# A recurrence feeding two mixtures on one core: a later third group, banks by use, border decays as one row, decode in halves

## The chip, the core and the metric

The kernel is one program on one core of a Trainium2 chip. The metric is device time in microseconds (us), the median of the runs shown. The engines are TensorE (PE, with its weight load PEld), VectorE (DVE), ScalarE (ACT), GpSimd (POOL) and SyncE (SP), each with its own queue, worked through in order. All transfers here are issued from SP's queue. SBUF holds tiles of 128 partitions; sums of matmuls lie in PSUM, in eight banks of 512 fp32 numbers per partition.

## The reference

A gated linear recurrence with a complex decay makes `y`, which becomes `x` of two feed-forward layers, one behind the other:

```python
for t in range(S):                                  # B, H, S, D = 4, 8, 768, 48
    new_re = ar * S_re - ai * S_im                  # decay, its magnitude clipped at 0.999
    new_im = ar * S_im + ai * S_re
    S_re, S_im = new_re + k[t] (x) v[t], new_im
    y[t] = q[t] . S_re
x = y as 3072 tokens x 384
h = x @ w_in                                        # 384 -> 2048
g = where(h > 0, h, exp(min(h, 0)) - 1)
x = g @ w_out                                       # 2048 -> 384
h = max(x @ w1, x @ w2, x @ w3)                     # 384 -> 768
out = h @ w_out2                                    # 768 -> 384
```

## The kernel before

**Stages.** The 3072 steps are cut into 12 groups of 256, each of two chunks of 128. A group's recurrence is a chain of small operations on all engines: logarithms and angles of the decay (`sq`, `m2`, `inv1`, `inv2`, `rho`, `lnr`), their running sums by matmul (`cum_t`, `cum_l`), exponentials and sines, the rotated `q` and `k` (`emul`, `hat`), their transposes (`tr_pe`, `tr_evac` for the first three groups, DVE transposes and DMAs after these), scores (`score`, `mask`), the state handed from chunk to chunk (`gain`, `state`, `state_out`), and the output (`yout`, `x_split`). `x_split` writes the 256 tokens as a high and a low part, since each fp32 product is made of three products of such parts.

Block b of the first layer has the tokens of group b. It takes eight steps (b, j), j = 0 to 7: `h_pair` (line 699, 18 matmuls) makes 256 hidden features, `elu` and `elu_split` (ACT and DVE, lines 79, 710, 84 and 719) turn them into a high and a low part, and two steps later `o_pair` (line 742, 18 matmuls) adds them into three banks x0 to x2. When a block is done, `x2_out` copies these banks and writes them to DRAM (`x2d`). Behind all twelve blocks comes the second layer (lines 948 and 972).

**Weights.** A weight arrives as 64-bit words, and `dec1` decodes each of its 16 tiles once: three integer passes on DVE (lines 202, 206 and 209), a rounding copy on ACT (line 84) and a subtraction on DVE (line 216). Step (0, j) needs tiles 2j and 2j + 1.

**What sets the order.** The steps are in a list: three of block 0, then blocks 1 and 0 in turn, then block by block; block 2 begins at place 16. Group n's chain has a table `STEPS` of relative times from -31 to -2, and each entry becomes an event at `due[n]` + r x `a`, where `due[n]` is the place of (n, 0), and `a` the pace. An event runs when the list of steps has come to its time. A scheduler then places all instructions on their engines by these priorities and its own estimate of when each is ready.

**Banks.** x0 to x2 hold the output sums, three banks (tag h) the hidden features, and two (tag a) all sums of the recurrence. `apsum` hands the two out in strict turn; an instruction that gets a bank whose sum is still to be read waits for the reader.

**Border decays.** A chunk's state is scaled by the decay at the border to the next chunk, for which `gain` writes three rows to DRAM (`gd`): one of `em`, one of `ep`, one of a rate. They come back with heads and features exchanged (`f`, 96 x 24), and DVE multiplies them there (lines 415 and 416).

Of the kernel before, what the change touches and what calls it, by code (L numbers as in the profile page):

```python
# [20 lines left out]
P = 128  # L21
# [72 lines left out]
def tile_kernel(  # L94
# [30 lines left out]

    early, banks_a = [0, True], []

    def apsum():
# [4 lines left out]
        return apsum_a()  # L133

    def apsum_a():

        if not banks_a:
            banks_a.extend(ps.tile([P, 512], F32, tag="a", name="a", bufs=2) for _ in (0, 1))
        banks_a.reverse()
        return banks_a[0]  # L140

# [22 lines left out]
    for i in (0, 2):  # L164
        raw = at([P, 4 * P], "p", bufs=2)[:, :(4 - i) * P]
        a, b = (3 * P + 2, 7 * P + 2) if i == 0 else (8 * P + 2, 10 * P + 2)
        nc.sync.dma_start(raw, consts[:, a:b])
        nc.gpsimd.tensor_copy(sums_r[:, i + i:4 + i].rearrange("p a t -> p (a t)"), raw)
    tri_l = [sums_r[:, i] for i in (0, 1)]
# [18 lines left out]
    x2d = dp.tile([NT // P, P, NK * P], F32, name="x2d")  # L188
    gd = dp.tile([2 * NG, 3, W], F32, name="gd")

# [54 lines left out]

    s_full = [at([P, 4, P], f"s{i}") for i in (0, 1)]
    s_tiles = [s[:96] for s in s_full]
    rates = [s.rearrange("p a t -> p (a t)")[96:128, :W] for s in s_full]
    for s in s_tiles:
# [75 lines left out]
    def bslice(c):  # L325
        return slice(96, 128) if c == 0 else slice(0, 32)

    def halves(n, x, k):

        if n < TRI_R:  # L330
            return
        T["halves"] = t = at([P, 2, W], "gs", F32R)
# [5 lines left out]
    def cumsum(n, tri, tri_r, x):  # L338
        bank = apsum()
        if n < TRI_R:  # L340
            nc.tensor.matmul(bank[:, :W], lhsT=tri, rhs=x, start=True, stop=True)
            return bank
        for i in (0, 1):
            nc.tensor.matmul(  # L344
                bank[:, :W], lhsT=tri_r, rhs=T["halves"][:, i], start=i == 0, stop=i == 1
            )
        return bank

    def halves_t(n, c):
        halves(n, T["th", n][:, c, :], -0.5 / math.pi)  # L350

    def halves_l(n, c):
        halves(n, T["lnr", n][:, c, :], 1.0)

    def cum_t(n, c):
        T["tps", n, c] = cumsum(n, tri_t[c], keep_r[c], T["th", n][:, c, :])

    def nr(n, c):
        bank = T.pop(("tps", n, c))
# [26 lines left out]
    def cum_l(n, c):  # L386
        T["lps", n, c] = cumsum(n, tri_l[c].bitcast(F32), tri_l[c], T["lnr", n][:, c, :])

    def cum_lx(n, c):
        bank = T.pop(("lps", n, c))  # L390
        ep, em = at([P, W], f"ep{c}"), at([P, W], f"em{c}")
        T["ep", n, c], T["em", n, c] = ep, em
        act.activation(ep, bank[:, :W], AF.Exp)
        act.activation(em, bank[:, :W], AF.Exp, scale=-1.0)

    def rate(n):
        for c in (0, 1):
            act.activation(rates[c], T["lnr", n][bslice(1 - c), c, :], AF.Exp, scale=0.5)

    def gain(n, c):  # L400
        if ends(n, c):
            return
        n2, c2 = after(n, c)
        row, off = (P - 1, 31) if c == 0 else (0, 0)
        ci = 2 * n + c
        for i, x in enumerate((T["em", n2, c2], T["ep", n, c])):
            nc.sync.dma_start(gd[ci, i:i + 1], x[row:row + 1, :])
        nc.sync.dma_start(gd[ci, 2:3], rates[c2][off:off + 1, :])
        f = at([96, 3, H], "f", bufs=2)
        for j in (0, 1):  # L410
            T["dma"] = nc.sync.dma_start(
                f[j * D:(j + 1) * D], gd[ci].rearrange("o (h d) -> d o h", h=H)
            )
        g = at([96, H], "g", bufs=2)
        nc.vector.tensor_tensor(out=g, in0=f[:, 0], in1=f[:, 1], op=ALU.mult)
        nc.vector.tensor_tensor(out=g, in0=g, in1=f[:, 2], op=ALU.mult)
        T["g", ci] = g
# [67 lines left out]
    def tr_evac(n, c, x, hf):  # L485
        if n >= PE_TR:
            return
        act.copy(
            T["qkt", n, c][x][:, 4 * hf:4 * hf + 4],
            T.pop(("trb", n, c, x, hf))[:96, :].rearrange("p (i t) -> p i t", i=4),  # L490
        )
# [22 lines left out]
    def score(n, c, hf):  # L514
        T["sc", n, c, hf] = bank = apsum()
        kt, qt = T["kt", n, c], T["qt", n, c]
# [11 lines left out]
    def mask(n, c, hf):  # L528
        bank = T.pop(("sc", n, c, hf))
        t = at([P, 4, P], "p", bufs=2)  # L530
# [27 lines left out]
    def state_out(n, c):  # L558
        ci = 2 * n + c
        if ends(n, c):  # L560
            return
        sp = T["sps", ci][:96, :W].rearrange("p (j r e) -> p j r e", j=4, r=2)
        new = split_heads(s_tiles[(ci + 1) % 2])
# [48 lines left out]
    def x_split(n, c):  # L612
        ci = 2 * n + c
        xt = x_tile(n)
        sl = slice(c * P, (c + 1) * P)
        y = T.pop(("y", n, c))[:, :W].rearrange("p (k t) -> p k t", k=NK)
        act.copy(xt[:, 0, :, sl], y)
# [136 lines left out]
    def x2_out(b):  # L754
        t = mp.tile([P, NK, BT], F32, tag="dt", name="x2", bufs=1)
        for m in range(NK):
            act.copy(t[:, m], T["x2", b][m])
        dst = x2d[2 * b:2 * b + 2].rearrange("c p (m t) -> p m c t", m=NK)
        for m in range(NK):
            nc.sync.dma_start(dst[:, m], t[:, m].rearrange("p (c t) -> p c t", t=P))  # L760

    def dec1(f):
        if f % 2:
            t = at([P, NWB], "tb")[:, :NWA]
        else:
            t = mp.tile([P, NWA], F32, tag="dt", name="dt", bufs=1)
        w1[f] = decode(wp, raw[f], NWA, f"w{f}", t)

# [59 lines left out]
    for t in (apsum_a(), apsum_a()):  # L828
        nc.tensor.matmul(t, lhsT=zero[:, :P], rhs=zero, start=True, stop=True)

    def both(f, *a):
# [65 lines left out]
    for n in range(1, NG):  # L897
        for r in STEPS:
            for half in (0, 1):
                events.append((due[n] + (r + half / 2) * a, n, r, half))  # L900
        if n + 1 < NG:
            a = min(SPAN, due[n + 1] - due[n] + a * (-FIRST - NP)) / -FIRST
# [444 lines left out]
```

## Time and profile before

| | |
|---|---|
| median of 3 runs | 923.98 us (923.41 to 925.28) |
| profiled execution | 924.66 us, of which 922.9 is the span from first to last instruction |
| busy in the span | PE 879.2 us (95%), DVE 584.8 (63%), ACT 535.8 (58%) |
| mean granted TensorE clock | 0.985 of full speed |

Busy times are a mean over stages with different limits, so the sections below go by stage. A wait is put down to the instruction that ended it.

### The profile page before, as it was taken

What the parts mean: (1) busy time and instruction counts of PE and PEld (TensorE: products, weight loads), DVE (VectorE), ACT (ScalarE), POOL (GpSimd) and SP (SyncE); (2) the same over time, 40 slices, a digit from 0 to 9 for tenths busy, and PEclk for the clock granted to TensorE, in tenths of its full rate; (3) what the DMA queues carried; (4) which work ended last, traced back from release to release, by engine and by line L of the source; (5) the groups of instructions that cost most, each with busy time, mean ns of one, the idle gap of its engine ahead of it and who ended that gap; (6) DMA issues with size and microseconds to landing.
All of it is one profiled execution on the core that took longest, in us unless ns stands there. A gap on an engine that the chain in (4) does not pass through costs nothing.

```text
span 922.9 us, 21089 instructions
## 1 busy us (share of the span) xinstructions
PE 879.2 (95%) x8968; PEld 797.4 (86%) x8968; DVE 584.8 (63%) x952; ACT 535.8 (58%) x869; POOL 1.2 (0%) x6
## 2 busy tenths in 40 slices
PE   6577999999999999999999999999999999999996
PEld 2455989999999999999999999998898989898886
DVE  5888898877877787878786643969734141413220
ACT  7958787686867675758664533746858421211121
POOL 0000000000000000000000000000000000000000
PEclk9977999999999999999999999999999999999999
DMA  9763022443433443443343323429778210000001
GB/s 329 255 224 87 11 43 85 103 103 93 98 92 98 102 89 114 75 121 76 99 83 91 53 59 100 182 93 369 259 280 308 78 35 34 1 35 1 19 17 38
DMA packets 100655, 102.21 MB, mean 111 GB/s; under 512 B 53516, under 2 KB 83528, under 8 KB 99784
## 3 DMA queue, kind: packets, MB, share of 16 engines
q1 hardware_dynamic: 100552, 100.77, 36.6%
q8 instruction: 72, 1.18, 0.5%
q14 instruction: 31, 0.25, 0.1%
HBM read 77.06 MB, written 9.53 MB: 94 GB/s over the span
## 4 chain that ended last, share of the span: by engine, by line
PE 81%; ACT 9%; DVE 6%; issue 1%; SPq 1%; DMA 1%; DVEq 0%; ACTq 0%
PE mb L948 24%; PE x L742 19%; PE h L699 18%; PE ob L972 8%; PE a L581 4%; PE a L522 3%; ACT L79 3%; ACT aux L79 1%; PE a L549 1%; PE a L344 1%; ACT e L79 1%; SPq L508 1%; ACT m L79 1%; PE a L483 1%; ACT g L84 1%
## 5 line engine op out<-in xcount | busy, mean ns | idle before, releaser
L699 PE MATMUL h<-x,w 128*128 128x256 f32 x1728 | 231.8, 287 | 2.5 <-ACT w L84 1.4
L742 PE MATMUL x<-g,w 128*128 128x256 f32 x1728 | 230.4, 286 | 0.5 <-DVE g L719 0.5
L948 PE MATMUL mb<-xx,w 128*128 128x512 f32 x972 | 224.8, 392 | 0.0
L699 PEld LDWEIGHTS h<-x,w 128*128 128x128 f32 x1728 | 217.2, 193 | 7.1 <-ACT w L84 1.6
L742 PEld LDWEIGHTS x<-g,w 128*128 128x128 f32 x1728 | 215.1, 191 | 6.6 <-issue 3.8
L948 PEld LDWEIGHTS mb<-xx,w 128*128 128x128 f32 x972 | 182.4, 188 | 40.8
L79 ACT ACTIVATE e<-h 128x512 f32<-128x512 f32 x96 | 57.0, 594 | 91.4 <-PE h L699 91.3
L710 DVE SCALAR_TENSOR_TENSOR e<-e,h 128x512 f32<-128x512 f32 x96 | 65.3, 681 | 44.8 <-ACT e L79 44.8
L84 ACT CAST g<-e 128x512 fp32r<-128x512 f32 x96 | 59.2, 617 | 49.1 <-DVE e L710 49.0
L956 DVE TENSOR_TENSOR t<-mb,t 128x512 f32<-128x512 f32 x36 | 24.9, 690 | 97.8 <-PE mb L948 97.8
L719 DVE TENSOR_TENSOR g<-e,g 128x512 fp32r<-128x512 f32 x96 | 65.6, 684 | 28.6 <-ACT g L84 28.5
L972 PE MATMUL ob<-w,m 128*128 128x384 f32 x432 | 76.4, 337 | 0.0
L972 PEld LDWEIGHTS ob<-w,m 128*128 128x128 f32 x432 | 75.6, 188 | 0.5
L84 ACT CAST m<-t 128x512 fp32r<-128x512 f32 x36 | 22.3, 619 | 92.0 <-DVE t L957 91.9
L79 ACT ACT_TABLE_LOAD x54 | 69.3, 1283 | 1.7 <-PEq L1331 0.7
L79 ACT ACTIVATE e<-e 128x512 f32<-128x512 f32 x96 | 60.7, 632 | 2.1
L957 DVE TENSOR_TENSOR t<-mb,t 128x512 f32<-128x512 f32 x36 | 24.9, 691 | 36.1 <-PE mb L948 36.1
L522 PE MATMUL a<-qkt 96*32 96x128 f32 (+3 forms) x1536 | 38.0, 244 | 3.0 <-ACT qkt L84 2.3
L522 PEld LDWEIGHTS a<-qkt 96*32 96x32 f32 x1536 | 32.3, 112 | 9.5 <-ACT qkt L84 2.6
L84 ACT COPY o<-ob 128x384 f32<-128x384 f32 x24 | 11.4, 475 | 45.6 <-PE ob L972 45.6
L960 DVE TENSOR_TENSOR m<-t,m 128x512 fp32r<-128x512 f32 x36 | 24.9, 691 | 19.7 <-ACT m L84 19.7
L532 DVE TENSOR_TENSOR p<-a,sums_r 128x512 f32<-128x512 f32 x48 | 32.7, 683 | 7.0 <-PE a L522 5.9
(106 smaller groups left out, 923.3 us busy)
## 6 DMA issues: line engine op xcount, KB each, us to landing
qkt<-tb SPq DMA_DIRECT2D x216, 64.0 KB
raw<-in_wa_dram SPq DMA_DIRECT2D x16, 768.0 KB
again<-in_wa_dram SPq DMA_DIRECT2D x16, 768.0 KB
raw<-in_wb_dram SPq DMA_DIRECT2D x6, 1536.0 KB
v<-in_v_dram SPq DMA_DIRECT2D x24, 352.0 KB
q<-in_q_dram SPq DMA_DIRECT2D x12, 384.0 KB
k<-in_k_dram SPq DMA_DIRECT2D x12, 384.0 KB
x2d<-x SPq DMA_DIRECT2D x36, 128.0 KB
```

The lines of the kernel that those rows point to most:

```text
L79: ins = self.nc.scalar.activation(out, in_, func, **k)
L84: self.nc.scalar.copy(out, in_)
L522: nc.tensor.matmul(bank[32 * s:32 * s + 32, i * P + 32 * a:i * P + 32 * b], lhsT=k1[:, f], rhs=q1[:, a:b], start=True, stop=True, tile_pos ...
L532: nc.vector.tensor_tensor(out=t.rearrange("p (i e) t -> p i e t", e=2), in0=bank.rearrange("p (i e t) -> p i e t", i=2, e=2), in1=keep[c], ...
L581: nc.tensor.matmul(bank[32 * quad:32 * quad + 32, o * P:(o + 1) * P], lhsT=lhs, rhs=rhs, start=start, stop=stop, tile_position=(0, 32 * quad),
L699: nc.tensor.matmul(bank[:, i * BT:(i + 1) * BT], lhsT=w[:, wi, wsl], rhs=xb[b][:, xi, kk, :], start=m == 0, stop=m == 8,)
L710: nc.vector.scalar_tensor_tensor(out=e, in0=e, scalar=-1.0, in1=bank, op0=ALU.add, op1=ALU.max)
L719: nc.vector.tensor_tensor(out=g[:, 1], in0=e, in1=g[:, 0].bitcast(F32), op=ALU.subtract)
L742: nc.tensor.matmul(x2[m], lhsT=w[:, wi, wsl], rhs=g[:, gi, i * BT:(i + 1) * BT], start=j + i + s == 0 and b > 1, stop=j == NP - 1 and i == ...
L948: nc.tensor.matmul(bank, lhsT=wbt[f][:, wt, o:o + P], rhs=x[:, xi, kk].rearrange("p c t -> p (c t)"), start=m == 0, stop=m == 8,)
L956: nc.vector.tensor_tensor(out=t, in0=banks[1], in1=t, op=ALU.max)
L972: nc.tensor.matmul(bank[:, :DM], lhsT=mt[:, mi, ts], rhs=wbt[f][:, wt, NWB - DM:], start=f == 0 and s == 0, stop=f == NF2 - 1 and s == 2,)
```

## The change

- `apsum` keeps a list `live` of banks whose sums are still to be read; `take` strikes a bank off when the instruction that reads it is written. `apsum` gives the bank of the two that isn't live, and where both are, one of the three of tag h.
- The group n = 2 (the third) gets a pace of its own, `due[2] / 31`, so its first event falls on time 0 and not before it.
- `rate` writes into a tile of its own, `gt`; `gain` multiplies it by `em` and `ep` on 32 partitions (the border row is one of them), sends one row to DRAM and reads back 96 x 8.
- `halves` and `cumsum` pass their tile by a key, as do others; the running sums are the same.
- Odd and even weight tiles are decoded in the two halves of one tile (`tb`), not in two tiles.
- `x2_out` uses two tiles of the pool of `elu` (tag e), where it had one of its own of three thirds.

```diff
-        banks_a.reverse()
-        return banks_a[0]
+        b = banks_a[0] if banks_a[0] not in live else banks_a[1]
+        if b in live:
+            assert not stays, "both banks hold sums that are still to be read"
+            return ps.tile([P, 512], F32, tag="h", name="a", bufs=3)
+        banks_a.remove(b)
+        banks_a.append(b)
+        live.append(b)
+        return b
+
+    def take(*key):
+        b = T.pop(key)
+        if b in live:
+            live.remove(b)
+        return b
...
     def rate(n):
+        T["gt", n] = t = at([P, W], "gt")
         for c in (0, 1):
-            act.activation(rates[c], T["lnr", n][bslice(1 - c), c, :], AF.Exp, scale=0.5)
+            sl = bslice(1 - c)
+            act.activation(t[sl], T["lnr", n][sl, c, :], AF.Exp, scale=0.5)
...
-        row, off = (P - 1, 31) if c == 0 else (0, 0)
+        sl = bslice(c)
+        t = T["gt", n2]
+        nc.vector.tensor_tensor(out=t[sl], in0=t[sl], in1=T["em", n2, c2][sl], op=ALU.mult)
+        nc.vector.tensor_tensor(out=t[sl], in0=t[sl], in1=T["ep", n, c][sl], op=ALU.mult)
+        row = P - 1 if c == 0 else 0
         ci = 2 * n + c
-        for i, x in enumerate((T["em", n2, c2], T["ep", n, c])):
-            nc.sync.dma_start(gd[ci, i:i + 1], x[row:row + 1, :])
-        nc.sync.dma_start(gd[ci, 2:3], rates[c2][off:off + 1, :])
-        f = at([96, 3, H], "f", bufs=2)
+        nc.sync.dma_start(gd[ci], t[row:row + 1, :])
+        g = at([96, H], "g", bufs=2)
         for j in (0, 1):
             T["dma"] = nc.sync.dma_start(
-                f[j * D:(j + 1) * D], gd[ci].rearrange("o (h d) -> d o h", h=H)
+                g[j * D:(j + 1) * D, :], gd[ci].rearrange("o (h d) -> d (o h)", h=H)
             )
-        g = at([96, H], "g", bufs=2)
-        nc.vector.tensor_tensor(out=g, in0=f[:, 0], in1=f[:, 1], op=ALU.mult)
-        nc.vector.tensor_tensor(out=g, in0=g, in1=f[:, 2], op=ALU.mult)
...
     def score(n, c, hf):
-        T["sc", n, c, hf] = bank = apsum()
+        T["sc", n, c, hf] = bank = apsum(n > 0)
...
     def x2_out(b):
-        t = mp.tile([P, NK, BT], F32, tag="dt", name="x2", bufs=1)
-        for m in range(NK):
-            act.copy(t[:, m], T["x2", b][m])
         dst = x2d[2 * b:2 * b + 2].rearrange("c p (m t) -> p m c t", m=NK)
         for m in range(NK):
-            nc.sync.dma_start(dst[:, m], t[:, m].rearrange("p (c t) -> p c t", t=P))
+            if m != 1:
+                t = mp.tile([P, 2, BT], F32, tag="e", name="x2", bufs=2)
+            act.copy(t[:, m % 2], T["x2", b][m])
+            nc.sync.dma_start(dst[:, m], t[:, m % 2].rearrange("p (c t) -> p c t", t=P))
+
+    words = []
 
     def dec1(f):
-        if f % 2:
-            t = at([P, NWB], "tb")[:, :NWA]
-        else:
-            t = mp.tile([P, NWA], F32, tag="dt", name="dt", bufs=1)
-        w1[f] = decode(wp, raw[f], NWA, f"w{f}", t)
+        if not words:
+            words.append(at([P, 2, NWA], "tb"))
+        w1[f] = decode(wp, raw[f], NWA, f"w{f}", words[0][:, f % 2])
...
-                events.append((due[n] + (r + half / 2) * a, n, r, half))
+                pace = due[n] / -FIRST if n == 2 else a
+                events.append((due[n] + (r + half / 2) * pace, n, r, half))
```

How the instructions stand is shown at three places. In the changed kernel the lines below 123 have moved by 10 to 16; `m_472` before and `m_844` after are the tile of the third group's squared magnitude.

On DVE, before, these rows stand between the rotated operands of the second group's first chunk (`qh`, `kh`, with one decoding row behind them) and the third group's first operation there (`m_472`):

```order
L216 TENSOR_TENSOR w<-tb,w 128x768
L202 TENSOR_SCALAR dt<-raw 128x768
L202 TENSOR_SCALAR tb<-raw 128x768
L206 SCALAR_TENSOR_TENSOR dt<-raw,dt 128x768
L206 SCALAR_TENSOR_TENSOR tb<-raw,tb 128x768
L209 SCALAR_TENSOR_TENSOR dt<-raw,dt 128x768
L209 SCALAR_TENSOR_TENSOR tb<-raw,tb 128x768
L216 TENSOR_TENSOR w<-dt,w 128x768
L202 TENSOR_SCALAR dt<-raw 128x768
L287 TENSOR_TENSOR m_472<-aux,m_472 128x768
```

On DVE after the change, the rows behind the same two operands:

```order
L421 TENSOR_TENSOR gt<-gt,em_494 32x384
L467 TENSOR_TENSOR q<-q,ep_493 128x384
L422 TENSOR_TENSOR gt<-gt,ep_478 32x384
L467 TENSOR_TENSOR k<-k,em_494 128x384
L724 SCALAR_TENSOR_TENSOR e<-e,h 128x512
L474 TENSOR_TENSOR qh<-q,cs 128x768
L228 TENSOR_TENSOR w<-tb,w 128x768
L218 SCALAR_TENSOR_TENSOR tb<-raw,tb 128x768
L733 TENSOR_TENSOR g<-e,g 128x512
L221 SCALAR_TENSOR_TENSOR tb<-raw,tb 128x768
L474 TENSOR_TENSOR kh<-k,cs 128x768
```

The second chunk's operands and the first `elu` now stand ahead of the next tiles' decoding; `m_844` comes 15 rows further down, behind the second group's first `x_split`.

On PE, before, from the middle of the first hidden features to the second group's transposes (`cst` and `qh` or `kh`), with the state sums (`v`, `kh`) between:

```order
L699 MATMUL h<-x,w 128x256 x25
L483 MATMUL a<-cst,qh 96x128 x4
L699 MATMUL h<-x,w 128x256 x16
L549 MATMUL a<-v,kh 32x48 x13
L483 MATMUL a<-cst,qh 96x128 x4
L549 MATMUL a<-v,kh 32x48 x11
L483 MATMUL a<-cst,kh 96x128 x8
```

On PE after the change, the same place:

```order
L713 MATMUL h<-x,w 128x256 x17
L497 MATMUL a<-cst,qh 96x128 x8
L497 MATMUL a<-cst,kh 96x128 x4
L713 MATMUL h<-x,w 128x256 x2
L497 MATMUL a<-cst,kh 96x128 x4
L756 MATMUL x_119<-g,w 128x256
```

The third step's hidden matmuls no longer stand between the transposes but behind them, and the first output matmuls stand close by.

On SP, before, at the end of a later block (`x2d` is the block's output, `qkt` the next group's transposes):

```order
L265 DMA k<-in_k_dram 128x768
L760 DMA x2d<-x_2804 128x2x128 x3
L144 DMA re<-in_a_re_dram 128x768
```

On SP after the change:

```order
L275 DMA k<-in_k_dram 128x768
L774 DMA x2d<-x_2775 128x2x128 x2
L774 DMA x2d<-x_2780 128x2x128
L156 DMA re<-in_a_re_dram 128x768
```

The three writes leave from two tiles, of which the second has a place of its own in the pool of `elu`.

## Rows read from the trace of the kernel before

**Rows 1.** The page's 40 slices: busy tenths, granted clock in tenths.
```profile
PE   6577999999999999999999999999999999999996
PEclk9977999999999999999999999999999999999999
```

**Rows 2.** Windows by stage: stretch and length; busy of PE, PEld, DVE, ACT, POOL; clock, DMA.
```profile
60.00:82.50 22.50, 12.00 (x163) 9.81 (x164) 19.59 (x30) 16.53 (x24) 0.00 (x0) 0.62 0.20 35
...
95.00:172.00 77.00, 74.24 (x866) 69.78 (x865) 69.65 (x115) 63.08 (x98) 0.00 (x0) 1.00 0.20 49
...
172.00:616.50 444.50, 441.45 (x5897) 424.53 (x5896) 326.23 (x550) 284.02 (x452) 0.00 (x0) 1.00 0.38 96
616.50:923.00 306.50, 299.34 (x1406) 257.71 (x1404) 111.88 (x162) 115.90 (x214) 0.00 (x0) 0.99 0.32 115
```

**Rows 3.** Who PE waited for from 50 to 100 us: total, times, longest.
```profile
PE a L483 <- ACT em L79: 5.7, 1, 5.7
PE a L483 <- ACT qkt L84: 3.5, 2, 2.1
```

**Rows 4.** Timeline: start, length, instruction, count, idle before it and what ended that.
```profile
61.23 0.95 DVE L216 TENSOR_TENSOR w<-dt,w 128x768 fp32r<-128x768 f32 x1
...
62.10 0.95 DVE L216 TENSOR_TENSOR w<-tb,w 128x768 fp32r<-128x768 f32 x1
...
66.63 0.83 ACT L84 CAST w<-dt 128x768 fp32r<-128x768 f32 x1 [4.82 <-DVE dt L209]
67.36 0.84 ACT L79 ACTIVATE m<-re 128x768 f32<-128x768 f32 x1
...
69.67 1.28 ACT L79 ACT_TABLE_LOAD   x1
...
71.36 0.48 ACT L79 ACTIVATE em<-a 128x384 f32<-128x384 f32 x1
...
71.89 1.09 PE L483 MATMUL a<-cst,qh 128*96 128x128 f32 x4 [5.70 <-ACT em L79]
```

**Rows 5.** Windows from one DVE row to another, columns as in rows 2.
```profile
26.62:95.64 69.02, 50.08 (x793) 40.54 (x794) 61.96 (x99) 52.60 (x76) 0.00 (x0) 0.83 0.51 167
95.64:172.17 76.53, 73.77 (x861) 69.31 (x861) 69.18 (x114) 62.49 (x96) 0.00 (x0) 1.00 0.20 49
```

**Rows 6.** DVE's groups by shape: count, busy us, mean ns, idle before and its end.
```profile
L381 DVE SCALAR_TENSOR_TENSOR th<-nr,cst,th 32x384 f32<-32x384 f32 x20 | 12.2, 611 | 0.5
...
L303 DVE TENSOR_TENSOR re<-re,aux 128x768 f32<-128x768 f32 x11 | 10.5, 958 | 9.8 <-ACT aux L79 9.7
...
L415 DVE TENSOR_TENSOR g<-f 96x8 f32<-96x8 f32 x20 | 3.1, 157 | 3.6 <-DMA f<-gd 3.5 <-issue 0.2
```

**Rows 7.** Timeline: the ends and marks of the stretches, columns as in rows 4.
```profile
26.62 0.95 DVE L460 TENSOR_TENSOR qh<-q,cs 128x768 f32<-128x768 f32 x1
...
95.00 4.36 PE L699 MATMUL h<-x,w 128*128 128x256 f32 x35
...
95.64 0.69 DVE L719 TENSOR_TENSOR g<-e,g 128x512 fp32r<-128x512 f32 x1
...
168.03 0.51 DVE L618 SCALAR_TENSOR_TENSOR x<-a,x 128x384 fp32r<-128x384 f32 x1
...
170.28 2.32 PE L699 MATMUL h<-x,w 128*128 128x256 f32 x18
...
172.17 0.69 DVE L719 TENSOR_TENSOR g<-e,g 128x512 fp32r<-128x512 f32 x1
```

**Rows 8.** Timeline at the ends of two later blocks, columns as in rows 4.
```profile
229.78 0.65 ACT L84 COPY x<-x 128x256 f32<-128x256 f32 x2
229.92 0.69 DVE L719 TENSOR_TENSOR g<-e,g 128x512 fp32r<-128x512 f32 x1 [1.24 <-ACT g L84]
...
231.07 2.42 PE L742 MATMUL x<-g,w 128*128 128x256 f32 x18
...
277.17 0.69 DVE L719 TENSOR_TENSOR g<-e,g 128x512 fp32r<-128x512 f32 x1
...
278.66 2.31 PE L742 MATMUL x<-g,w 128*128 128x256 f32 x18
```

More of the change, by code (lines that the diff above doesn't have):

```diff
@@ L124, in at, with apsum @@
         return ap.tile(shape, dt, tag=tag, name=name or tag, bufs=bufs)
-    early, banks_a = [0, True], []
-    def apsum():
+    early, banks_a, live = [0, True], [], []
+    def apsum(stays=False):
         if early[1]:
@@ L132, in apsum, with apsum_a @@
                 return ps.tile([P, 512], F32, tag="h", name="a", bufs=3)
-        return apsum_a()
-    def apsum_a():
+        return apsum_a(stays)
+    def apsum_a(stays=False):
         if not banks_a:
             banks_a.extend(ps.tile([P, 512], F32, tag="a", name="a", bufs=2) for _ in (0, 1))
-        banks_a.reverse()
-        return banks_a[0]
+        b = banks_a[0] if banks_a[0] not in live else banks_a[1]
[11 more added lines that the diff above has]
+        return b
     def load_re(n):
@@ L164, in tile_kernel @@
     for i in (0, 2):
-        raw = at([P, 4 * P], "p", bufs=2)[:, :(4 - i) * P]
+        part = at([P, 4 * P], "p", bufs=2)[:, :(4 - i) * P]
         a, b = (3 * P + 2, 7 * P + 2) if i == 0 else (8 * P + 2, 10 * P + 2)
-        nc.sync.dma_start(raw, consts[:, a:b])
-        nc.gpsimd.tensor_copy(sums_r[:, i + i:4 + i].rearrange("p a t -> p (a t)"), raw)
+        nc.sync.dma_start(part, consts[:, a:b])
+        nc.gpsimd.tensor_copy(sums_r[:, i + i:4 + i].rearrange("p a t -> p (a t)"), part)
     tri_l = [sums_r[:, i] for i in (0, 1)]
@@ L188, in tile_kernel @@
     x2d = dp.tile([NT // P, P, NK * P], F32, name="x2d")
-    gd = dp.tile([2 * NG, 3, W], F32, name="gd")
+    gd = dp.tile([2 * NG, 1, W], F32, name="gd")
     def load_w(pool, src, f, n, tag):
@@ L244, in decode_any @@
         return split_w(wpool, t, n, tag)
-    s_full = [at([P, 4, P], f"s{i}") for i in (0, 1)]
-    s_tiles = [s[:96] for s in s_full]
-    rates = [s.rearrange("p a t -> p (a t)")[96:128, :W] for s in s_full]
+    s_tiles = [at([96, 4, P], f"s{i}") for i in (0, 1)]
     for s in s_tiles:
@@ L326, in bslice, with halves @@
         return slice(96, 128) if c == 0 else slice(0, 32)
-    def halves(n, x, k):
+    def halves(n, x, k, *key):
         if n < TRI_R:
             return
-        T["halves"] = t = at([P, 2, W], "gs", F32R)
+        T[key] = t = at([P, 2, W], "gs", F32R)
         nc.vector.tensor_scalar(out=t[:, 0], in0=x, scalar1=k, scalar2=None, op0=ALU.mult)
@@ L336, in halves, with cumsum @@
         )
-    def cumsum(n, tri, tri_r, x):
+    def cumsum(n, tri, tri_r, x, *key):
         bank = apsum()
@@ L342, in cumsum @@
             return bank
+        t = T.pop(key)
         for i in (0, 1):
             nc.tensor.matmul(
-                bank[:, :W], lhsT=tri_r, rhs=T["halves"][:, i], start=i == 0, stop=i == 1
+                bank[:, :W], lhsT=tri_r, rhs=t[:, i], start=i == 0, stop=i == 1
             )
@@ L349, in halves_t @@
     def halves_t(n, c):
-        halves(n, T["th", n][:, c, :], -0.5 / math.pi)
+        halves(n, T["th", n][:, c, :], -0.5 / math.pi, "ht", n, c)
     def halves_l(n, c):
-        halves(n, T["lnr", n][:, c, :], 1.0)
+        halves(n, T["lnr", n][:, c, :], 1.0, "hl", n, c)
     def cum_t(n, c):
-        T["tps", n, c] = cumsum(n, tri_t[c], keep_r[c], T["th", n][:, c, :])
+        T["tps", n, c] = cumsum(n, tri_t[c], keep_r[c], T["th", n][:, c, :], "ht", n, c)
     def nr(n, c):
-        bank = T.pop(("tps", n, c))
+        bank = take("tps", n, c)
         r = at([P, W], "gs")
@@ L386, in cum_l @@
     def cum_l(n, c):
-        T["lps", n, c] = cumsum(n, tri_l[c].bitcast(F32), tri_l[c], T["lnr", n][:, c, :])
+        T["lps", n, c] = cumsum(
+            n, tri_l[c].bitcast(F32), tri_l[c], T["lnr", n][:, c, :], "hl", n, c
+        )
     def cum_lx(n, c):
-        bank = T.pop(("lps", n, c))
+        bank = take("lps", n, c)
         ep, em = at([P, W], f"ep{c}"), at([P, W], f"em{c}")
@@ L489, in tr_evac @@
             T["qkt", n, c][x][:, 4 * hf:4 * hf + 4],
-            T.pop(("trb", n, c, x, hf))[:96, :].rearrange("p (i t) -> p i t", i=4),
+            take("trb", n, c, x, hf)[:96, :].rearrange("p (i t) -> p i t", i=4),
         )
@@ L528, in mask @@
     def mask(n, c, hf):
-        bank = T.pop(("sc", n, c, hf))
+        bank = take("sc", n, c, hf)
         t = at([P, 4, P], "p", bufs=2)
@@ L561, in state_out @@
             return
-        sp = T["sps", ci][:96, :W].rearrange("p (j r e) -> p j r e", j=4, r=2)
+        sp = take("sps", ci)[:96, :W].rearrange("p (j r e) -> p j r e", j=4, r=2)
         new = split_heads(s_tiles[(ci + 1) % 2])
@@ L615, in x_split @@
         sl = slice(c * P, (c + 1) * P)
-        y = T.pop(("y", n, c))[:, :W].rearrange("p (k t) -> p k t", k=NK)
+        y = take("y", n, c)[:, :W].rearrange("p (k t) -> p k t", k=NK)
         act.copy(xt[:, 0, :, sl], y)
@@ L829, in tile_kernel @@
         nc.tensor.matmul(t, lhsT=zero[:, :P], rhs=zero, start=True, stop=True)
+    live.clear()
     def both(f, *a):
```

## The prediction

> **What bounds the kernel now.** I read the page's slices first: PE is at nine tenths or more from the fifth slice to the last but one, and lower in the first four, where the granted clock falls too [rows 1]. So a change in order can give something back only in the first 100 us or so. The windows put sizes on this. From 172 us to 616.5, where the second layer begins, PE is busy for 441.45 of 444.5 us, and from there to the end for 299.34 of 306.5; these two stretches leave 10 us, of which the 7 at the end have nothing to do with the edits. From 60 to 82.5 us PE is busy for 12.0 us only, at a granted clock of 0.62 of full speed on average, so between its two levels of 1.2 and 2.4 GHz: 10.5 us are idle, and of the 12.0 some 4.6 are lost to the clock (12.0 x 0.38) [rows 2].
>
> Who is waited for there: PE's longest wait, 5.7 us, is for the second group's `em`, since the transpose needs the bank that `em` reads, and another 3.5 us go to two waits for copies of earlier transposes [rows 3]. The timeline shows why `em` is late: ACT sits idle for 4.82 us until DVE has decoded a tile, and does the third group's `m` and a table load of 1.28 us before it comes to `em` at 71.36; PE starts 0.5 us later [rows 4]. So the stall is PE's, its cause the order on DVE and ACT.
>
> DVE is the second resource to look at. I take the stretch from DVE's first rotated operand at 26.62 us to the sixteenth second half of `elu_split` (line 719) at 172.17, close to where block 2 begins on PE (170.28) [rows 7]. DVE is busy for 61.96 us of the first 69.02 and for 69.18 of the other 76.53, so it idles 7.06 and 7.35 us, together 14.4 [rows 5]. PE has 18 us to give back from 60 to 172 us (15.1 as above and 2.8 idle after 95), DVE only 14.4, less what the change adds to it. The smaller one is the cap.
>
> **The change part by part.** *The third group later.* In the new order its first DVE operation (`m`, line 287) stands behind the second group's first `x_split`, not ahead of the fourth pair's end. At the third `elu_split` half (95.64 before) DVE has then done less: six decode passes, five operations of 768 columns, three short passes, an `x_split` and smaller ones. Two wide rows follow each other 0.87 us apart [rows 4], a little under their length, and I use such steps throughout: 11 x 0.87 + 3 x 0.47 + 0.55 + 0.53 + six small products at 0.12 = 12.8 us less, and six products of the border more, 3.2. That is 9.6 us of work put off, not saved: every one of these operations has come back by the sixteenth half.
>
> *Border decays.* Each border has two products of 32 x 384 more and two of 96 x 8 less. The nearest row of the first is line 381 on the same 32 partitions, 0.611 us long [rows 6], a step of 0.53; of the second, 0.157, a step of about 0.11. Up to the sixteenth half there are twelve of the new ones (6.4 us) against ten of the old (1.1); two operations that were ahead of it (0.87 and 0.27) now stand behind. DVE has 4.1 us more to do. In the whole kernel it is 20 x 0.85 = 17 us, but behind 172 us DVE is busy for 326 of 444.5 and the rest takes it in. What it saves: DVE waited for `f` for 3.5 us in all [rows 6], in five places behind 170 us, where PE is the bound. I count nothing. If all of it were on the path, it would be 3.5; if the products push PE into waits, it is the last rival.
>
> *Banks.* The 5.7 us wait goes, since the transpose gets a bank that has been read. In its place three of the four transposes come one behind another in one bank, as the other holds the state's sum, so each waits for the copy ahead of it: about 0.6 for the transposes and 0.6 for the copy, 2.4 us of PE's time. It lies beside DVE's work, which is what ends last there, so its price is nothing; were PE the bound, it would be these 2.4.
>
> *Decode in halves* has the same four DVE passes and one copy a tile; the halves change places as the two tiles did. Nothing.
>
> *The block's output in `elu`'s tiles.* The third copy of a block waits until the second half of the split ahead of it is done. At two ends of blocks that half is done at 230.61 and 277.86; a copy takes 0.33, and PE needs the third bank six matmuls (0.72 us) behind its start at 231.07 and 278.66 [rows 8]. That leaves 0.85 and 1.2 us to spare. Nothing, as long as DVE is no later than that.
>
> *The sum.* DVE needs 131.1 + 4.1 = 135.2 us from 26.62, so without any wait it is at the sixteenth half at 161.9, 10.3 us earlier. I went along the new order of DVE, ACT and PE with the durations of the rows, and find 3.6 us of waits on DVE up to about 93 us, the largest, 1.35, at line 303 for ACT's `aux` (before, these eleven operations waited 9.7 in all [rows 6]). On that walk PE starts the 36 hidden matmuls that stood at 95.0 [rows 7] at some 84.5. From there DVE has 70 us of work for PE's 69.3 until block 2, and starts 7 us behind it, so it seldom waits for PE; for ACT's chains I set 1.5 us, and 1 for the clock. So the half comes at 161.9 + 6.1 = 168.0, 4.2 us early. PE gains a little more, since at 170.28 it was 1.7 us behind its operand, `x_split`'s second half, which ended at 168.54 [rows 7], and will now be close behind it: between 4.2 and 5.9, and I take 5.5. Nothing behind 172 us gives it back, since PE is full there. The profiled execution took 924.66 us; 919.2 is left. That execution is 0.7 above the median, so the median goes to 918.5.
>
> On the clock, the traces show full speed from 82.5 us on, after PE had become busy at about 79, and the walk leaves PE sparse once more from 69 to 84 us, so its 36 matmuls (4.36 us) may start at the lower level; that is the 1 us above. The Trainium skill, in "TensorE: Matmul & The Clock Gate", section "Part 1: The HAM clock gate", says that the array is throttled by default and that activity releases it. By that rule shorter stalls alone bring no clock back, and the sum is the one above; if the clock stayed up, it would be 1 us less.
>
> **The rivals.** *DVE hardly waits (0.15).* With PE ahead and ACT at 63 of 77 us, DVE could run nearly full: a lead of 10.3 + 1.7 gives 912 at the median. For it speaks that DVE is the later one all through; against it the waits of rows 6.
>
> *Paid back (0.14).* The 9.6 us put off fall into the stretch from 95 us, where DVE idled 7.35 us and may do so again, since its waits there are for ACT and hardly for PE. Then the waits are 3.6 + 7.35, the half is early by 14.4 - 10.95 - 4.1 = -0.7, and with PE's 1.7 the gain is 1.0: 923.0, within 0.2%.
>
> *Late splits (0.11), the slower side.* Block ends: if the split's second half comes over 1.0 us later against PE than before (the mean of the two margins), PE waits for the third bank. DVE's two more products a border and its later groups can do that. At 2 us later it is 1.0 us at each of ten ends: 919.2 + 10 = 929.2, at the median 928.5. It decides from 1.5 us late on, where it takes the gain. Against it: DVE has 27% of its time free there, and PE's new order at these places is the old one.
>
> *It doesn't do what it says (0.04).* The transposes could find both banks held after all and take hidden banks; the order shows one such case in all, so little can come of it: 920 to 924.
>
> **How the numbers follow.** The forecast, 918.5, has 0.56, with 915.5 to 921.5 as its own range (waits of 3 to 9 us in place of 6.1). A run of this kernel can tell 0.2%, 1.85 us. Faster by more than that: forecast, the full gain, and a part of the two mild cases, 0.77. Within: 0.11. Slower: the late splits and some for what I don't see, 0.12. The range of 911 to 925 holds all but the late splits and a few in a hundred below.
>
> **What would show it.** Right: PE's wait for `em` at 66 to 72 us is gone; the 36 hidden matmuls begin at 83 to 87; DVE is over 95% busy from 40 to 93 us; block 2 begins on PE at 164 to 166; behind it the two traces run alike, 5 to 6 us apart. Wrong: DVE idle for more than 6 us from 95 us to the sixteenth half; PE waits at line 742 for ACT's copies at the block ends; a lead that shrinks behind 172 us; or a lead over 8, which would mean that DVE was not what bound this stage.

## The result, and the profile of the changed kernel

The changed kernel takes 932.2 us (median of 4 runs, 931.4 to 933.38) against 924.62 of the kernel before (4 runs, 923.41 to 925.28): ratio 1.0081, 95% interval 1.0067 to 1.0095, so 7.6 us slower. The forecast was 918.5, with 911 to 925 as its range. The profiled execution took 931.75 us; its span is 930.0, 7.1 more than before.

The page's slices of the changed kernel, against [rows 1]:

```profile
PE   5688879999999999999999999999999999999996
PEclk9889989999999999999999999999999999999998
```

The third and fourth slice are fuller than before (8 where 7 stood), but the fifth and sixth (93 to 140 us) are lower, 8 and 7 where 9 stood, and the clock falls in the sixth. Windows by stage of the changed kernel, columns as in [rows 2]:

```profile
60.00:82.50 22.50, 20.80 (x383) 17.65 (x383) 19.89 (x30) 16.17 (x25) 0.00 (x0) 0.90 0.35 104
...
95.00:120.00 25.00, 20.63 (x145) 18.73 (x144) 21.26 (x30) 22.66 (x30) 0.00 (x0) 0.93 0.09 32
120.00:145.00 25.00, 16.73 (x180) 14.75 (x181) 22.39 (x36) 22.87 (x34) 0.00 (x0) 0.83 0.09 16
145.00:175.00 30.00, 30.00 (x448) 28.28 (x442) 26.00 (x45) 20.01 (x33) 0.00 (x0) 0.97 0.27 79
```

The old stall is gone: from 60 to 82.5 us PE is busy for 20.80 us at a clock of 0.90, where it had 12.00 at 0.62. But from 95 to 145 it idles for 4.37 + 8.27 = 12.6 us, where [rows 2] leave 2.8 idle in all of 95 to 172, and its clock there falls below full speed, which it held before. Who is waited for, in the changed kernel from 95 to 175 us (in all, times, longest):

```profile
PE x L756 <- ACT g L84: 4.8, 1, 4.8
PE a L351 <- DVE th L392: 2.1, 1, 2.1
PE a L355 <- ACT qkt L84: 2.0, 1, 2.0
PE x L756 <- DVE g L733: 2.0, 2, 1.5
PE a L351 <- DVE nr L375: 1.7, 1, 1.7
```

`th` and `nr` are links of the third group's chain. DVE's longest waits in the changed kernel from 95 us to the sixteenth half of the split (175.74):

```profile
DVE g L733 <- ACT g L84: 2.6, 2, 1.9
DVE th L392 <- ACT th L79: 1.8, 1, 1.8
DVE e L724 <- ACT e L79: 1.4, 2, 1.2
```

DVE's windows from its first rotated operand (25.85) to 95 us, and from there to that half, columns as in [rows 5]:

```profile
25.85:95.00 69.15, 57.87 (x884) 48.63 (x885) 65.76 (x101) 52.08 (x76) 0.00 (x0) 0.92 0.47 168
95.00:175.74 80.74, 68.10 (x766) 62.50 (x765) 70.39 (x110) 66.27 (x96) 0.00 (x0) 0.92 0.16 44
```

DVE is busy for 136.2 us and idle for 3.4 up to 95 us, as the walk had it (135.2 and 3.6). Behind 95 us it is idle for 10.35 us; the walk had 2.5. So the half comes at 175.7, not at 168. The timeline of PE gives the begin of block 2, which was at 170.28 in the kernel before [rows 7]:

```profile
174.32 2.32 PE L713 MATMUL h<-x,w 128*128 128x256 f32 x18
```

That is 4.0 us later. The other 3.1 us of the 7.1 are lost behind it: from there to the second layer it is 449.1 us (to 623.4), and it was 446.0 (170.28 to 616.3). PE's longest waits from 175 us to the second layer:

```profile
PE x L756 <- ACT x L84: 2.5, 4, 0.9
PE a L355 <- DVE gs L343: 1.6, 1, 1.6
```

The first is the wait for the copies at block ends, which the prediction's sum set at nothing.

### The profile page after: what moved, and what is told of

Same layout as the page of the kernel before. It is cut to its first block, busy times and chain, and to the rows that moved or that the text cites. A ratio compares the mean times of both kernels' runs of the same rounds, so it can differ in the third digit from the quotient of the medians.

```text
span 930.0 us, 21061 instructions
## 1 busy us (share of the span) xinstructions
PE 882.2 (95%) x8968; PEld 799.4 (86%) x8968; DVE 602.3 (65%) x952; ACT 541.5 (58%) x871; POOL 1.2 (0%) x6
## 4 chain that ended last, share of the span: by engine, by line
PE 76%; ACT 9%; DVE 9%; issue 2%; DMA 1%; SPq 0%; DVEq 0%; ACTq 0%
PE mb L964 24%; PE x L756 17%; PE h L713 17%; PE ob L988 8%; PE a L595 4%; ACT L79 3%; PE a L536 2%; PE a L563 2%; ACT aux L79 1%; PE a L355 1%; ACT e L79 1%; ACT cs L79 1%; DVE w L228 1%; DMA raw<-in_wb_dram 1%; PE a L497 1%
## 5 line engine op out<-in xcount | busy, mean ns | idle before, releaser
L756 PE MATMUL x<-g,w 128*128 128x256 f32 x1728 | 234.0, 288 | 10.1 <-ACT g L84 5.6
L713 PE MATMUL h<-x,w 128*128 128x256 f32 x1728 | 235.1, 287 | 2.2 <-DVE x L632 1.9
L756 PEld LDWEIGHTS x<-g,w 128*128 128x128 f32 x1728 | 217.7, 193 | 17.3 <-ACT g L84 6.0
```

The lines of the kernel that those rows point to most:

```text
L713: nc.tensor.matmul(bank[:, i * BT:(i + 1) * BT], lhsT=w[:, wi, wsl], rhs=xb[b][:, xi, kk, :], start=m == 0, stop=m == 8,)
L756: nc.tensor.matmul(x2[m], lhsT=w[:, wi, wsl], rhs=g[:, gi, i * BT:(i + 1) * BT], start=j + i + s == 0 and b > 1, stop=j == NP - 1 and i == ...
```

## The experiments

Medians stand beside the difference to the kernel before in the same comparison, then the ratio and its 95% interval. "Idle" is DVE's idle time from its first rotated operand to 95 us, plus that from there to the sixteenth half, worked out from such windows as above. "Less than the changed kernel" compares these differences, since each comparison has its own runs of the kernel before; the changed kernel's is +7.6.

### One part undone, or alone

**e1_old_pace**

```diff
-                pace = due[n] / -FIRST if n == 2 else a
+                pace = a
```

> The changed kernel, with the third group's places set as before (its chain begins before the first step, not at it); banks, border products, decode and x2_out as changed. Theory A, the later chain: the third group's links now fall at 95 to 145 us beside the fourth group's, with fewer hidden matmuls between two links, so PE waits for the links (3.8 us at 99 to 106 and 6.2 at 128 to 135 in the changed kernel); without it those waits go, the third group's work at 60 to 95 us comes back, and what is left of the change gives 918 to 925 us. Rival B, the border products: 4.1 us more DVE work up to 172 us are the loss; they are still here, so 929 to 933. Rival C, the banks: transposes one behind another in one bank make PE and ACT wait (2.0 us for qkt at 140); still here, so 929 to 933.

926.9 us, +1.9 (1.0018, 1.0007 to 1.0029). This lies between the ranges of A and of B and C. It is 5.7 less than the changed kernel: the later places are most of the loss. Idle 4.6 + 6.2. The timeline gives the begin of block 2:

```profile
170.26 2.32 PE L713 MATMUL h<-x,w 128*128 128x256 f32 x18
```

That is where it was before the change, so what the places cost lies ahead of it (4.0 us in the changed kernel). Behind it this kernel's profiled execution loses 3.1 us, as the changed one's does (its second layer begins at 619.4), and that is not the places.

**e2_only_pace**

```diff
-                events.append((due[n] + (r + half / 2) * a, n, r, half))
+                pace = due[n] / -FIRST if n == 2 else a
+                events.append((due[n] + (r + half / 2) * pace, n, r, half))
```

> The kernel before, with the third group's later places alone. Theory A: slower than before, 928 to 936, with PE waits for the third group's links between 95 and 145 us. Rivals B and C: the later chain is harmless by itself and frees DVE before 95 us: 918 to 925.

930.16 us, +5.2 (1.0051, 1.0038 to 1.0065). With banks in strict turn a state sum gets the bank of the fourth group's first angle sum before that is read, so this group's angles are others; the work is the same. Idle 5.8 + 11.9. Theory A holds for the places.

**e3_only_banks** (`live`, `take` and the new `apsum` in the kernel before, as in the diff ahead)

> The kernel before, with banks handed out by whether they have been read, and nothing else. Theory A and rival B: the 5.7 us wait for em goes, and DVE and ACT set what is left of it: 918 to 924.5. Rival C: slower, 927 or more, with waits of PE for copies of transposes.

925.18 us, +0.2 (1.0001, 0.9990 to 1.0011): the same. No theory had that, and the reason stands in PE's waits from 50 to 100 us of this kernel:

```profile
PE a L495 <- ACT em L79: 6.9, 1, 6.9
PE a L495 <- ACT qkt L84: 3.9, 3, 2.1
```

The wait for `em` is still there. The operand of these transposes was done long before, as the timeline shows:

```profile
57.96 0.95 DVE L472 TENSOR_TENSOR qh<-q,cs 128x768 f32<-128x768 f32 x1
...
69.83 0.48 ACT L79 ACTIVATE em<-a 128x384 f32<-128x384 f32 x1
...
70.37 1.09 PE L495 MATMUL a<-cst,qh 128*96 128x128 f32 x4 [6.95 <-ACT em L79]
```

So they wait for a bank. `take` strikes a bank off the list when its reader is written, not when it has run: a bank whose reader still stands in ACT's queue is handed out as free.

**e4_border_x2** (border products, `gt`, decode and `x2_out` of the change, in the kernel before)

> The kernel before, with the border's products ahead of one row's transfer, and decode and x2_out in their new tiles (without these the border's tile does not fit); places and banks as before. Theory A and rival C: the work is hidden behind 172 us, and up to there it costs at most its 4.1 us: 923 to 928, with no PE wait over 3 us that the kernel before does not have. Rival B: 929 to 933, as much as the whole change loses.

926.44 us, +1.5 (1.0012, 1.0001 to 1.0023). DVE does 135.5 us of work up to the sixteenth half (131.1 before) and is yet there at 170.5, 1.6 us earlier, as it idles for 3.3 + 5.3 only. PE's waits of this kernel from 50 to 95 us have no `em` any more:

```profile
PE a L521 <- DVE s L568: 2.4, 1, 2.4
PE a L482 <- DVE qh L459: 2.0, 1, 2.0
```

The border products need `em` early; e7 below, which has the other two parts without them, keeps the wait (6.9 us). So it is the border product that brings `em` forward. Behind 172 us PE waits 1.9 us for copies at block ends and 2.9 us once for DVE's `gs` (0.9 in two places before), and gives the gain back.

**e7_only_x2dec** (decode in halves and `x2_out` in `elu`'s tiles, in the kernel before)

> The kernel before, with decode in halves of a tile and x2_out in elu's tiles alone. The border products with these two cost 1.4 us, and with them PE waited for three block-end copies, 1.9 us in all. If that wait belongs to x2_out's new tiles: 925.5 to 927. If it belongs to the border's work on DVE, which makes the splits late: 924 to 925.5, with no wait of PE for those copies.

926.73 us, +1.4 (1.0019, 1.0006 to 1.0033), with 0.6 us of waits for block-end copies. The cost of e4 belongs to these two, not to the border, though only a part of it shows as waits for those copies.

**e8_border_pool** (as e4, with these two lines changed)

```diff
-        nc.vector.tensor_tensor(out=t[sl], in0=t[sl], in1=T["em", n2, c2][sl], op=ALU.mult)
-        nc.vector.tensor_tensor(out=t[sl], in0=t[sl], in1=T["ep", n, c][sl], op=ALU.mult)
+        nc.gpsimd.tensor_tensor(out=t[sl], in0=t[sl], in1=T["em", n2, c2][sl], op=ALU.mult)
+        nc.gpsimd.tensor_tensor(out=t[sl], in0=t[sl], in1=T["ep", n, c][sl], op=ALU.mult)
```

> The kernel before with the border's products ahead of one row's transfer, decode and x2_out as changed, and the two products of 32 rows on GpSimd in place of VectorE. If VectorE's added 17 us are what the border costs: 924 to 925.5, the 1.4 us gone or a small gain, since up to 172 us VectorE has 6.4 us less to do than with them. If GpSimd is slow enough that the state's update waits for the border's row: 927 or more, with waits of the state's product for the row's transfer.

931.61 us, +6.3 (1.0063, 1.0050 to 1.0077). GpSimd's products are long, and DVE's own beside them too. The timeline of both engines in this kernel:

```profile
26.98 1.49 POOL L406 TENSOR_TENSOR gt<-gt,em 32x384 f32<-32x384 f32 x1 [18.25 <-ACT em L79]
27.53 1.76 DVE L459 TENSOR_TENSOR kh<-k,cs 128x768 f32<-128x768 f32 x1
28.55 1.60 POOL L407 TENSOR_TENSOR gt<-gt,ep 32x384 f32<-32x384 f32 x1
29.21 1.35 DVE L452 TENSOR_TENSOR k<-k,em 128x384 f32<-128x384 f32 x1
...
114.36 8.69 POOL L406 TENSOR_TENSOR gt<-gt,em 32x384 f32<-32x384 f32 x1 [45.28 <-ACT em L79]
```

Without GpSimd `kh` takes 0.95 us and `k` 0.55. The state then waited for the border's row (1.8 us of DVE in two places).

### The delay

**e6_mid_pace**

```diff
-                pace = due[n] / -FIRST if n == 2 else a
+                pace = 0.6 if n == 2 else a
```

> The changed kernel with the third group's first event at place -2.6, halfway between its old place (-5.2) and its new one (0). If the loss grows with the delay (A1 and A2), 927.5 to 931, between the 926.9 of the old place and the 932.2 of the new one. If one crossing of two operations does it, it is at one of the two ends: within 1 of 926.9 or of 932.2.

919.35 us, -6.0 (0.9938, 0.9923 to 0.9954): faster than both kernels, and outside every case of the expectation. Its windows of PE over the same stretches, its DVE windows to the sixteenth half (166.64), and the begin of block 2:

```profile
95.00:120.00 25.00, 22.64 (x209) 20.51 (x208) 22.28 (x32) 23.58 (x32) 0.00 (x0) 1.00 0.15 47
120.00:145.00 25.00, 22.35 (x278) 20.35 (x278) 24.81 (x42) 22.48 (x35) 0.00 (x0) 1.00 0.09 17
...
26.66:95.00 68.34, 57.91 (x872) 47.90 (x873) 66.65 (x102) 55.09 (x79) 0.00 (x0) 0.95 0.48 168
95.00:166.64 71.64, 66.62 (x792) 61.23 (x791) 67.83 (x108) 64.02 (x95) 0.00 (x0) 1.00 0.17 50
...
163.54 2.32 PE L713 MATMUL h<-x,w 128*128 128x256 f32 x18
```

DVE idles for 1.7 + 3.8 us. That is close to the forecast's sum: 6.1 us of waits, the half at 168, block 2 at 164 to 166.

**e16_pace64** (as e6, with `0.64`)

> The changed kernel with the third group's first event at place -3.8, between the old place (926.9 us) and -2.6 (919.35). If the gain comes evenly with the delay: 921.5 to 924.5. If an order of two operations decides: within 1.5 of 919.35 or of 926.9.

927.44 us, +3.3 (1.0042, 1.0027 to 1.0057), as at the old place. So the delay doesn't act evenly: begins at -5.2, -3.8, -2.6 and 0 give 926.9, 927.4, 919.4 and 932.2.

**e9_mid_plain** (the kernel before, with `0.6` and a key for each group's halves)

> The kernel before, with the third group's first event at place -2.6 and a key for each group's halves, nothing else: old banks, old border, old decode and x2_out. If half of the delay is the whole gain and the other parts only cost their 1.4 us: 917 to 919.5. If the half delay gains only together with the banks (the transposes no longer wait for em) or the border: 922 to 926.

923.72 us, -0.9 (0.9990, 0.9981 to 0.9999). Half the delay alone gives little. Idle 7.5 + 5.4.

**e10_mid_banks** (as e9, with the new banks)

> The kernel before with the third group at -2.6, keys, and the new way to hand out banks; old border, decode and x2_out. At -2.6 the other parts together gave 4.4 us (923.7 without them, 919.35 with them). If the banks give it: 916.5 to 920, since the border and x2_out cost 1.4 by themselves. If the border's early products give it: 922 to 925.

923.41 us, -0.8 (0.9989, 0.9980 to 0.9998). The banks give nothing here either. What makes e6 4 to 5 us faster than e9 and e10 is the border with the two tiles; the idle time up to 95 us shows where: 1.7 against 7.5 and 7.2.

**e5_both_late** (`0.67 if n == 3` beside the full delay)

> The changed kernel, with the fourth group put off as well: its first event at place 3.2 in place of 0.3, so that its steps no longer stand beside the third group's. Theory A1, coincidence: the loss is that both groups' chains ask for DVE and ACT at 95 to 145 us at once; apart they cost less, 925 to 930. Theory A2, short links: the loss is that a group put off has fewer hidden matmuls between the links of its chain, whoever stands beside it; now the fourth has fewer as well and waits of its own at 130 to 180 us: 933 to 938.

932.86 us, +7.5 (1.0080, 1.0058 to 1.0102): no change in sum, but in place. The fourteenth half is 7.2 us earlier than in the changed kernel (153.2 against 160.4), and PE then waits 4.4 us at block ends. Neither A1 nor A2 is told by it.

**e11_fifth_late** (`0.74 if n == 4` beside the full delay)

> The changed kernel, with the fifth group's first event at place 9.1 in place of 6.4, so that its squares (m, aux: 1.6 us of ScalarE at 127 in the changed kernel) no longer stand in the run of 8.5 us that the elu copy waits behind. If these squares make the run too long: 925 to 930, PE's wait at 128 to 135 at most 4. If the third group's sines and sums alone fill it, or VectorE is what is late there: 931 to 934.

938.35 us, +13.8 (1.0154, 1.0136 to 1.0172). PE's wait for the elu copy falls from 4.8 to 1.8 us, but one of 3.8 us for its low part on DVE has come, and block 2 begins at 173.62, only 0.7 earlier: the squares hold the copy up, and are little of the loss. Behind 172 us PE has new waits (3.7 us for block-end copies, 2.8 for an `x_split`).

### The full delay, one order at a time

**e12_g_first**

```diff
-        act.copy(g[:, 0], e)
+        with tc.high_priority(offset=PRIO_X):
+            act.copy(g[:, 0], e)
```

> The changed kernel, with the copy of elu_split (g from e) given a higher priority; at the third group's sines it then stands seven operations of ScalarE earlier, and the rest of the orders stays nearly as it is. If ScalarE's order is the cause of PE's 6.2 us at 128 to 135: that wait goes, 925 to 927.5. If VectorE is full there and its decoded weights come at 134.8 all the same: PE does the 18 matmuls of the copy (2.3 us) in the gap and then waits for the weights, 928.5 to 931.

933.38 us, +8.8 (1.0099, 1.0085 to 1.0114). PE's longest waits from 95 to 175 us in this kernel:

```profile
PE a L497 <- DVE qh L474: 5.1, 1, 5.1
PE x L757 <- DVE g L734: 3.3, 2, 2.8
PE a L351 <- DVE th L392: 2.1, 1, 2.1
```

The copy is early now, but DVE comes to its low part late, and to the third group's `qh` later still. The wait of 4.8 us named ACT; the work that PE lacked stood in DVE's queue.

**e13_mid_g_first** (the same on e6)

> The changed kernel with the third group at -2.6 and the copy of elu_split at a higher priority. PE's waits for that copy and its low part were 2.5 us from 95 to 172 us at -2.6; if they end last there: 916.5 to 918.5. If not, as without it: 919 to 920.

920.1 us, -4.5 (0.9954, 0.9940 to 0.9968): nothing gained there either.

**e14_arctan_first**

```diff
-                events.append((due[n] + (r + half / 2) * pace, n, r, half))
+                late = -0.2 if (n, r, half) == (2, -21, 1) else 0.0
+                events.append((due[n] + (r + half / 2) * pace + late, n, r, half))
```

> The changed kernel, with one event moved by 0.2 of a place: the third group's arctangent window stands ahead of the fourth group's logarithms, as it does with every earlier begin of the third group, where the changed kernel has it behind them (logarithms at 97.1 to 100.0, arctangent only at 101.3). Theory X: this crossing holds up the third group's chain; with it undone, VectorE's wait of 1.8 and PE's of 3.8 us at 99 to 106 go, the chain is 4 to 5 us earlier, and 922 to 928 us come out. Rival Y: the chain is too late as a whole and VectorE is full from 113 us on; then PE's stall at 128 to 142 stays and 930 to 933 come out.

929.9 us, +5.7 (1.0060, 1.0047 to 1.0073), 1.9 less than the changed kernel. The timeline of the changed kernel shows the crossing that this undoes:

```profile
94.04 0.95 DVE L330 SCALAR_TENSOR_TENSOR lnr<-m,aux 128x768 f32<-128x768 f32 x1
95.03 0.85 ACT L79 ACTIVATE m<-re 128x768 f32<-128x768 f32 x1 [1.70 <-DVE lnr L330]
...
97.11 1.28 ACT L79 ACT_TABLE_LOAD   x1
98.40 0.85 ACT L79 ACTIVATE aux<-re 128x768 f32<-128x768 f32 x1
...
99.99 1.28 ACT L79 ACT_TABLE_LOAD   x1
101.28 0.84 ACT L79 ACTIVATE th<-th 128x768 f32<-128x768 f32 x1
...
102.16 0.61 DVE L392 SCALAR_TENSOR_TENSOR th<-nr,cst,th 32x384 f32<-32x384 f32 x1 [1.77 <-ACT th L79]
102.82 0.91 PE L351 MATMUL a<-th,cst 128*128 128x384 f32 x2 [2.12 <-DVE th L392]
```

The fourth group's squares (95.03) and logarithms (98.40) go ahead of the third group's arctangent (101.28), for which DVE and PE wait. In e14 the waits for `th` and `nr` are gone, DVE's idle time falls to 3.9 + 7.0, but PE still waits for the elu copy:

```profile
PE x L756 <- ACT g L84: 5.1, 1, 5.1
PE x L756 <- DVE g L733: 2.2, 2, 1.1
```

**e15_mid_crossed** (e6, with the fourth group's `m2` and logarithms moved ahead by 0.15 and 1.62 of a place, so that the crossing comes about)

> The changed kernel with the third group at -2.6 (919.35 us), and the fourth group's logarithms put ahead of the third group's arctangent, the crossing that the changed kernel has. Theory X: it loses a good part of what lies between 919.35 and 932.2: 923 to 929. Rival Y: 918.5 to 921.

921.51 us, -2.7 (0.9968, 0.9958 to 0.9979), 2.2 above e6 by the medians and 3.3 by the differences to the kernel before. Both e14 and e15 come out between the ranges of X and Y: the crossing acts both ways, but it is only 2 to 3 us of the 13 between half and full delay. The rest is left to Y, which no run tests by itself.

### Block-end copies

**e18_own3**

```diff
         for m in range(NK):
-            if m != 1:
-                t = mp.tile([P, 2, BT], F32, tag="e", name="x2", bufs=2)
-            act.copy(t[:, m % 2], T["x2", b][m])
-            nc.sync.dma_start(dst[:, m], t[:, m % 2].rearrange("p (c t) -> p c t", t=P))
+            if m == 0:
+                t = mp.tile([P, 2, BT // 2], F32, tag="x2", name="x2", bufs=1)
+                u = t.rearrange("p c t -> p (c t)")
+            else:
+                if m == 1:
+                    t = mp.tile([P, 2, BT], F32, tag="e", name="x2", bufs=2)
+                u = t[:, m - 1]
+            act.copy(u, T["x2", b][m])
+            nc.sync.dma_start(dst[:, m], u.rearrange("p (c t) -> p c t", t=P))
```

> The changed kernel, with the same x2_out (first third in a tile of its own), the third group at its full delay. If the block-end copies cost their waits (four, 2.5 us): 929 to 931, so about a third of the loss of 7.6 is theirs. If they only take the place of other waits: 931.5 to 933.

929.07 us, +4.5 (1.0050, 1.0036 to 1.0063), 3.1 less than the changed kernel. PE no longer waits for the copies; its longest waits from 175 us on that name a releaser:

```profile
PE a L563 <- ACT em L79: 0.4, 1, 0.4
PE x L756 <- ACT g L84: 0.3, 1, 0.3
```

The gain lies behind the begin of block 2, which is even later here than in the changed kernel:

```profile
176.59 2.32 PE L713 MATMUL h<-x,w 128*128 128x256 f32 x18
```

From there to the second layer it takes 445.2 us, against 449.1. The wait of 1.6 us for `gs` is down to 0.2 as well, so not all of this is shown to be the copies.

**e17_mid_own3** (the same on e6)

> The changed kernel with the third group at -2.6, and x2_out's first third of a block in a small tile of its own, the other two in one tile of elu: so the third copy no longer waits for a later half of the split. If the block-end copies cost what PE waits for them from 175 us on (three waits, 2.0 us): 917 to 918.5. If these waits only take the place of others: 918.8 to 920.

920.45 us, -4.2 (0.9951, 0.9938 to 0.9965). The waits are gone, but one of 2.1 us for a `mask` on DVE has come, and nothing is gained.

## Why the prediction was wrong

**The bound: right.** PE's stall at 60 to 82.5 us came from the order on DVE and ACT, and DVE was the cap. In the changed kernel the 36 hidden matmuls begin at 82.95 us (forecast 83 to 87), and DVE is busy for 50.07 of 53 us from 40 to 93 (94%, forecast over 95):

```profile
82.95 1.30 PE L713 MATMUL h<-x,w 128*128 128x256 f32 x9
85.22 3.49 PE L713 MATMUL h<-x,w 128*128 128x256 f32 x27 [0.97 <-DVE x L632]
...
40.00:93.00 53.00, 44.26 (x640) 37.13 (x629) 50.07 (x78) 38.46 (x57) 0.00 (x0) 0.94 0.47 170
```

**The sum: the failed step.** "From there DVE has 70 us of work for PE's 69.3 until block 2, and starts 7 us behind it, so it seldom waits for PE; for ACT's chains I set 1.5 us, and 1 for the clock." These 2.5 us were 10.35 of idle time on DVE. The walk went to about 93 us only; behind that a guess stood in its place. There the links of the third group, put off, stand in line with PE's own work: PE waits for `th`, `nr`, a `qkt` and the elu copy with its low part in its queue (12.6 us in all), hidden matmuls come late, and DVE in turn waits for that copy (2.6), for the arctangent (1.8) and for the elu (1.4). So block 2 came 4.0 us late, not 5.5 early. "Nothing behind 172 us gives it back" failed too, by 3.1 us; 9.5 + 3.1 are the 12.6 between the forecast for the profiled execution, 919.2, and its 931.75. The clock's 1 us stood in the wrong place: from 69 to 84 us, where the walk had PE sparse, the granted clock was 1.00. Behind that an estimate from the three windows from 95 to 175 us is 20.63 x 0.07 + 16.73 x 0.17 + 30.00 x 0.03 = 5.2 us lost at the lower of the two levels. The Trainium skill, in "TensorE: Matmul & The Clock Gate", section "Part 1: The HAM clock gate", says that the array's clock is throttled by default and that activity releases it; the windows agree, 0.83 where PE idles for 8.3 of 25 us, and 1.00 in e6, where it idles for 2.7.

**Put off, not saved: right in kind.** The rival "paid back" had the mechanism, work that comes back behind 95 us while DVE idles there, at a price too low: it let the old 7.35 us of idle time return, and it was 10.35. e6 shows that the forecast's own mechanism exists at half the delay, with its size (5.5 us of idle time against 6.1).

**Banks: wrong.** "The 5.7 us wait goes, since the transpose gets a bank that has been read." e3 keeps it with the new banks, and e4 loses it with the old ones: the bank handed out had a reader that was written and had not run. The border's early use of `em` takes the wait away. Its price of nothing in the sum holds, since e3 is the same as before.

**Border decays: right.** DVE has 5.0 us more to do up to the sixteenth half (forecast 4.1) and 17.5 in all (17), hidden: e4 less e7 is no loss.

**Block ends: mis-sized.** The step gave nothing "as long as DVE is no later than that". DVE was: ACT's copies waited 5.3 us in eight places for that half, PE 2.5 us at four ends, and e18, with the copies freed, is 3.1 us faster, of which 1.4 may be the `gs` wait that went too. The rival "late splits" had the mechanism at ten ends, for 10 us.

So both rivals came true at once: the later places cost about 5 us (5.7 undone, 5.2 alone; 4.0 ahead of block 2 in the profiled executions), `x2_out`'s tiles with the decode in halves 1.4 to 3.1 behind it, the banks and the border nothing by themselves. They don't add up exactly, since each changes the order that the others meet.

**Open.** The arctangent's crossing is 2 to 3 us; the rest of the 13 between half and full delay is named only as the third group's chain on a DVE queue without gaps (e12). Why a begin at -2.6 is 8 us better than one at -3.8 is not settled: DVE idles for 5.5 against 9.6 us, but no single crossing was found for it; block 2 is 5.4 us later there (168.93 against 163.54), and the rest lies behind it. Border and `x2_out` were not run apart at half the delay, since the border's tile does not fit without the other.

## What to carry to other kernels

Work that is put off has to be walked through to the place where it comes back, with the waits there, and not only up to the stall that it leaves. The engine that a wait names need not be the one to move: here a copy on ACT was named, and with the copy early PE waited as long for DVE's queue. Where a list of places decides the order, as here, try some values of a delay before judging it: here half of it gave 6.0 us and all of it lost 7.6.

## What was not expected

Products on GpSimd stretch DVE's beside them: `k` with `em` took 1.35 us in place of 0.55, and one of GpSimd's lasted 8.69 us, during which DVE's rows follow each other almost without a gap from 113.3 to 122.2 us (spans of GpSimd are rough). The Trainium skill, in "SBUF — State Buffer", section "SBUF: two separate sides", says that a DVE instruction with two SBUF inputs and a GpSimd instruction that reads SBUF share a port pair, which one of them holds to its end. The first rows agree: `k` ends at 30.56, 0.41 us behind GpSimd's row (30.15), and is 0.55 long by itself. The 8.69 us reach over many DVE instructions, which is more than that, and no run here shows why.

A long wait of PE does not always cost its clock: in e16 PE waited 3.0 us once at full clock, while the changed kernel went down to 0.83 in a window with a wait of 4.8.

With the third group at -2.6 or later and the others in their places, the fourth group's arctangent is issued twice, once in a window of its own and once beside the third group's sines, on the same tile (in the changed kernel's trace at 114.39 and 126.53 us). The rows of ACT in the changed kernel's order, with other rows between:

```
L79 ACTIVATE th_1154<-th_1154 128x768
L79 ACTIVATE th_1154<-th_1154 128x768
```

So this group's angles are the arctangent of an arctangent in these kernels: they do not compute quite what the kernel before does (at an angle of 0.1 the second arctangent takes off 0.0003). The second one takes 0.83 us of ACT; a window that skips a group already turned was not tried.
